# A two-headed SSM kernel on one core: inverse transform as 64 and 32 points, last stage on two groups at once, eight skips moved from TensorE to VectorE, and a new order of all work

## Chip, core and metric

The kernel runs on one core of one Trainium2 chip. The metric is the device time of one execution in microseconds (us). The engines are named as in the profile: PE (TensorE matmul; PEld its weight loads), DVE (VectorE), ACT (ScalarE), POOL (GpSimd) and SP (SyncE, which here only issues DMAs).

## What is computed

Two heads, whose outputs stand side by side. Head A is a diagonal complex recurrence over 2048 steps with 640 states; head B is a causal convolution over 2048 steps, done in the reference by FFT, of 640 channels, between two products.

```python
# A: x [1, 2048, 640]
Lam_bar = exp(dt * Lam);  B_bar = ((Lam_bar - 1) / Lam)[:, None] * Bmat
Bu = einsum("bld,pd->blp", x, B_bar)
h_t = Lam_bar * h_{t-1} + Bu_t                       # all t
a = 2 * einsum("blp,dp->bld", h, Cmat).real + x * Dskip
# B: q, k, v [1, 2048, 640]
kv = (sum of 4 shifted k * shift_k) * v
y = irfft(rfft(pad(kv, 4096)) * rfft(pad(ssm_k, 4096)))[:2048] + kv * ssm_D
b = q * y
out = concatenate([a, b], -1)                        # bfloat16
```

## The kernel before

**Head A.** Time is cut into 4 interleaved phases s (steps 4m + s), states into 5 blocks j of 128. `v{s}_{j}` (`pe_in`, L513) projects phase s of x, transposed as `xT{s}`, onto block j and adds the phase before it through diagonal matrices; `ve{s}_{j}` empties it from PSUM. Phase 0 then holds the input of a recurrence with a step of 4, which DVE does as a rotation (`rs`), a scan (`sc`) and a rotation back (`ra`, `rout`); `oa{s}_{j}` and `od{s}_{j}` carry its result to the other phases. `p{i}_{s}` (`pe_proj`, L571) is the output projection for rows i of phase s: two banks with 10 matmuls of 320 columns each, and then 3 small ones in each with a diagonal matrix of Dskip (`diagD`, L587), which add x * Dskip. `yo{i}_{s}` (L604) empties it on ACT, `yd{i}_{s}` (L607) stores it. C is brought in by two transposing DMAs (`CT0`, `CT1`) and scaled by `ca` (ACT) and `cs` (DVE).

**Head B.** Channels are cut into 5 groups G of 128. `kT`, `vT` are transposed loads; `tap` is the 4-step filter on PE, `kv` the product with v on DVE, `kvo` and `kvs` a trip to DRAM and back into another layout, `hs` the load of the filter's row (64 partitions at a time, pieces of 128 bytes). The transform runs in two stages: `s1h`/`s1k` (L662, 64 x 64 quarters of the array) and `s2h`/`s2k` (L675, two column halves), each emptied by `s1he`, `s1ke`, `s2he`, `s2ke`. `ya{G}_{half}` and `y{G}_{half}` (L687, L688, L693) are the product of the spectra on DVE. Then comes the way back. `inv{G}_{q}` (`pe_inv`, L695) takes 4 of 16 frequencies k1 with whole 128 x 128 matrices, four matmuls for each (real and imaginary part of in and out); `zs` empties 1024 columns into `Zs`; `zt{G}_{half}` (`turn_z`, L710) is a transposing DMA inside SBUF into `Zt`; `fin{G}_{half}` (`pe_fin`, L717) is the last stage, 16 matmuls with a moving matrix `Mq` of 64 columns; `ob{G}_{half}` (L725, DVE) multiplies by q, loaded by `qi{G}` (L715), and `od_{G}` (L730) stores the group.

**What sets the order.** `make_plan` gives each step its engine, its costs and what it needs; the costs steer nothing in the program that runs. `ORDER`, a list written out in full, is the sequence in which all steps are issued: each engine works through its own steps in this order and waits where a step's input is not there. `@n` names the PSUM bank pair, of which there are four, and a `!` puts a step on its other engine (an evacuation on DVE instead of ACT, a transposed copy on ACT, small parameters on POOL or SP).
SP's list is a queue too: a DMA whose input is late holds back all DMAs behind it.

Of the kernel before, what the change touches and what calls it, by code (L numbers as in the profile page):

```python
# [45 lines left out]
class Kernel:  # L46


    def __init__(self, ctx, tc, out, ins):
# [75 lines left out]
        t("qb", [128, 16, 128])  # L125
# [6 lines left out]
        self.Zt = self.zz[:, 4096:8192].rearrange("p (i b) -> p i b", i=32)  # L132
# [3 lines left out]
        self.tph = [flat(n).bitcast(i32).rearrange("p (q n) -> p q n", q=2) for n in (self.qb, self.kv_st)]  # L136
# [6 lines left out]
        self.diagG = self.H[:, 2].rearrange("p a b -> p (a b)")[:, 0:3 * n * 128].rearrange("p (s j d) -> p s j d", s=3, j=n)  # L143
# [46 lines left out]
    def pool_consts2(self):  # L190
# [3 lines left out]
        g.iota(self.c26[:], pattern=one, base=2 ** 26, channel_multiplier=0)  # L194
# [4 lines left out]
        g.iota(self.m_ph[:], pattern=[[1, 16]], base=0, channel_multiplier=0)  # L199

    def pool_consts3(self):
# [831 lines left out]
```

## Time and profile before

| What | Value |
|---|---|
| Median of 3 runs | 201.43 us (201.4 to 201.59) |
| The profiled execution | 201.36 us, its span 199.6 us |
| PE busy | 186.4 us (93%), weight loads 128.3 us |
| DVE busy | 164.9 us (83%) |
| ACT busy | 153.8 us (77%) |
| POOL busy | 24.8 us (12%) |
| DMA | 32.61 MB, mean 163 GB/s, 124908 packets, of them 120903 under 512 B |
| Longest waits | ACT for the projections (L604 on L587) 22.7 us in 10; DVE for the last stage (L725 on L720) 15.9 us in 2 |

The page calls an engine busy from the start of an instruction to its modelled end. Matmuls overlap in the pipeline: one of 128 columns reads as 219 ns, and the next begins 57 ns later. So the cost of a row of matmuls is read from the starts of what follows, not from the mean of one.

### The profile page before, as it was taken

What the parts mean: (1) busy time and instruction counts of PE and PEld (TensorE: products, weight loads), DVE (VectorE), ACT (ScalarE), POOL (GpSimd) and SP (SyncE); (2) the same over time, 40 slices, a digit from 0 to 9 for tenths busy, and PEclk for the clock granted to TensorE, in tenths of its full rate; (3) what the DMA queues carried; (4) which work ended last, traced back from release to release, by engine and by line L of the source; (5) the groups of instructions that cost most, each with busy time, mean ns of one, the idle gap of its engine ahead of it and who ended that gap; (6) DMA issues with size and microseconds to landing.
All of it is one profiled execution on the core that took longest, in us unless ns stands there. A gap on an engine that the chain in (4) does not pass through costs nothing. (4 is left out here: it accounts for less than half of the span.)

```text
span 199.6 us, 7503 instructions
## 1 busy us (share of the span) xinstructions
PE 186.4 (93%) x3328; PEld 128.3 (64%) x3340; DVE 164.9 (83%) x285; ACT 153.8 (77%) x189; POOL 24.8 (12%) x55
## 2 busy tenths in 40 slices
PE   7999999999989999999999998887999999999990
PEld 4444365544445456567777887677778887977770
DVE  5899877999999999999999999999999898420040
ACT  2499999988958998899998899799898983501321
POOL 8899561000000000000000000000000000000000
PEclk9999999999999999999999999999999999999998
DMA  4999999993586831985999786997995796597635
GB/s 112 209 221 217 207 266 214 210 192 85 90 174 163 164 50 27 240 163 86 236 188 194 121 167 126 157 254 140 194 155 150 158 164 153 126 175 176 143 130 138
DMA packets 124908, 32.61 MB, mean 163 GB/s; under 512 B 120903, under 2 KB 124236, under 8 KB 124876
## 3 DMA queue, kind: packets, MB, share of 16 engines
q1 hardware_dynamic: 124856, 32.13, 81.0%
q8 instruction: 26, 0.43, 0.9%
q14 instruction: 6, 0.05, 0.1%
q10 hardware_dynamic: 20, 0.01, 0.0%
HBM read 9.51 MB, written 7.86 MB: 87 GB/s over the span
## 5 line engine op out<-in xcount | busy, mean ns | idle before, releaser
L520 PE MATMUL ps<-xT,BT 128*128 128x512 bf16 x188 | 47.8, 381 | 0.9 <-DMA xT<-in_A_x_dram 0.3
L582 PE MATMUL ps<-Cs,hs 128*128 128x320 bf16 x240 | 36.3, 299 | 0.3 <-ACT Xs L467 0.3
L520 PEld LDWEIGHTS <-BT 128*128 128x128 bf16 x200 | 18.7, 98 | 22.6 <-issue 1.3
L604 ACT CAST BT<-ps 128x640 bf16<-128x640 f32 x16 | 10.9, 695 | 25.7 <-PE ps L587 22.7
L582 PEld LDWEIGHTS <-hs 128*128 128x128 bf16 x240 | 21.9, 98 | 7.9 <-issue 0.2
L725 DVE TENSOR_TENSOR qb<-ps,qb 128x1024 bf16<-128x1024 f32 x10 | 11.9, 1216 | 15.9 <-PE ps L720 15.9
L675 PEld LDWEIGHTS <-G 128*64 128x64 bf16 x640 | 19.1, 110 | 5.5 <-issue 4.1
L467 ACT CAST As_kv<-ps 128x1024 bf16<-128x1024 f32 x20 | 20.0, 1041 | 0.3 <-PE ps L662 0.3
L467 ACT CAST As_h<-ps 128x1024 bf16<-128x1024 f32 x20 | 19.8, 1040 | 0.0
L467 ACT CAST Hf<-ps 128x1024 bf16<-128x1024 f32 x19 | 19.3, 1042 | 0.0
L467 ACT CAST Xs<-ps 128x1024 bf16<-128x1024 f32 x19 | 18.8, 1031 | 0.0
L467 ACT CAST zz<-ps 128x1024 bf16<-128x1024 f32 x17 | 17.2, 1034 | 2.1 <-PE ps L704 2.1
L701 PE MATMUL ps<-Xs,H 128*128 128x128 bf16 x80 | 17.5, 219 | 0.9 <-ACT As_h L467 0.5
L703 PE MATMUL ps<-Xs,H 128*128 128x128 bf16 x80 | 17.5, 219 | 0.8 <-issue 0.8
L702 PE MATMUL ps<-Xs,H 128*128 128x128 bf16 x80 | 17.5, 219 | 0.4 <-DVE Xs L693 0.4
L704 PE MATMUL ps<-Xs,H 128*128 128x128 bf16 x80 | 17.5, 219 | 0.0
L693 DVE TENSOR_TENSOR Xs<-Xs,rot 128x1024 bf16<-128x1024 bf16 x20 | 12.9, 686 | 0.2
L687 DVE TENSOR_TENSOR rot<-Xs,Hf 128x2048 bf16<-128x2048 bf16 x10 | 12.2, 1220 | 0.8 <-ACT BT L604 0.5
L675 PE MATMUL ps<-As_kv,G 128*64 128x128 bf16 x320 | 11.7, 221 | 1.0 <-DVE vT L651 0.5
L688 DVE TENSOR_TENSOR Xs<-Xs,Hf 128x2048 bf16<-128x2048 bf16 x10 | 12.2, 1225 | 0.5
L675 PE MATMUL ps<-As_h,G 128*64 128x128 bf16 x320 | 11.7, 221 | 0.7 <-ACT Xs L467 0.7
L651 DVE TENSOR_TENSOR vT<-ps,vT 128x1024 bf16<-128x1024 f32 x10 | 11.9, 1213 | 0.4 <-PE ps L646 0.4
(204 smaller groups left out, 396.5 us busy)
## 6 DMA issues: line engine op xcount, KB each, us to landing
h_st<-in_B_ssm_k_dram SPq DMA_DIRECT2D x10, 256.0 KB, 4.2
kv_rows<-vT SPq DMA_DIRECT2D x5, 512.0 KB
kv_st<-kv_rows SPq DMA_DIRECT2D x10, 256.0 KB, 3.7
qb<-in_B_q_dram SPq DMA_DIRECT2D x5, 512.0 KB, 4.0
out_dram<-BT SPq DMA_DIRECT2D x16, 160.0 KB, 2.6
out_dram<-qb SPq DMA_DIRECT2D x5, 512.0 KB, 5.2
As_kv<-in_A_B_re_dram SPq DMA_DIRECT2D x3, 160.0 KB, 2.4
As_kv<-in_A_B_im_dram SPq DMA_DIRECT2D x3, 160.0 KB, 2.5
```

The source lines that it names most:

```text
L467: self.nc.scalar.copy(out=out, in_=in_)
L520: mm(o, lhsT=self.BT[:, r, k, j * 128:(j + 1) * 128], rhs=xT[:, k, :], start=(k == 0), stop=(s == 1 and k == NT - 1))
L582: mm(o[:, 0:320], lhsT=h[:, r, ts], rhs=self.Cs[:, r, j, c0:c0 + 320], start=(j == 0 and r == 0), stop=(not on_pe and j == NT - 1 and r == 1))
L651: self.nc.vector.tensor_tensor(out=self.vT[:, ts], in0=ps[:].rearrange("p a n -> p (a n)"), in1=self.vT[:, ts], op=ALU.mult)
L675: self.nc.tensor.matmul(o[64 * e:64 * e + 64, c:c + 128], lhsT=self.G[:, r, k, :], rhs=As[:, k, :], start=True, stop=True)
L687: tt(out=self.cross(), in0=X[:, ::-1, :], in1=self.Hf[:, 1:2, hs].to_broadcast([128, 2, 1024]), op=ALU.mult)
L688: tt(out=X, in0=X, in1=self.Hf[:, 0:1, hs].to_broadcast([128, 2, 1024]), op=ALU.mult)
L693: self.nc.vector.tensor_tensor(out=X[:, r, :], in0=X[:, r, :], in1=cr[:, r, :], op=ALU.add if r else ALU.subtract)
L701: mm(o_re, lhsT=self.H[:, 0, k1, :], rhs=yre, start=True, stop=False)
L702: mm(o_re, lhsT=self.H[:, 2, k1, :], rhs=yim, start=False, stop=True)
L703: mm(o_im, lhsT=self.H[:, 1, k1, :], rhs=yre, start=True, stop=False)
L704: mm(o_im, lhsT=self.H[:, 0, k1, :], rhs=yim, start=False, stop=True)
```

## The change

**The inverse** (`pe_inv`). The matrix `H` gets the layout [16 frequencies, 3, 64]: minus sine, cosine, sine of 64 points. Two neighbours of the three, 128 columns, are the weights of one matmul, which takes 64 rows of the spectrum (the even or the odd half e of the frequencies) and gives real and imaginary part for 64 points at once. Four matmuls for each k1 stay, each on half the rows; half e goes into its own PSUM bank. `zs` is now two copies of 512 columns. Half as many table entries are made (`H0`, `H1` in place of four), and the negated part is half as large. `diagG` gets a tile of its own instead of a part of `H`.

**The last stage** (`pe_fin`). `Mq` now has 2 x 32 x 4 entries, a real and an imaginary part with 32 points each. One piece takes 8 of the 32 blocks of `Zt` of two groups at once: the even group on column half 0 of the array, the odd one on column half 1, for each block and group two accumulating matmuls with 128 moving columns. Groups 0 and 1, and 2 and 3, go in four pieces together (`fin0_*`, `fin1_*`); group 4 goes alone in two (`fin2_*`), its channels split between the halves. For this `Zt` exists twice, the second time on top of `tabs`, whose last reader is `ra4`. `qb` holds two groups, 64 partitions each; loads and stores of q are 64 x 32 x 128 elements for a group, and for group 4 two DMAs of 64 x 32 x 64.

**The skips.** Eight projections, `SKV`, leave out the diagonal matmuls. For these x is loaded again, untransposed (`xs`, 160 KB each, three buffers), DVE multiplies it by Dskip (`xd`, bf16 in SBUF) and adds it when it empties PSUM (`yo` on DVE). The methods for this were there before and unused. The projections go in the order `PORD`; projection (1, 1) is done, emptied and stored by halves.

**The order.** `ORDER` is another list throughout. `lv3`, `lv1` and `lv4` (rows of parameters) go first on SP; `lam` and `gam` go to POOL.

```diff
+SKV = [(0, 1), (2, 3), (2, 0), (2, 1), (3, 3), (3, 2), (3, 1), (1, 3)]
+LAST = (1, 1)
-        t("H", [128, 3, 16, 128])
+        t("H", [128, 16, 3, 64])
-        t("qb", [128, 16, 128])
+        t("qb", [128, 32, 128])
-        self.Zt = self.zz[:, 4096:8192].rearrange("p (i b) -> p i b", i=32)
+        self.Zt = [f.rearrange("p (i b) -> p i b", i=32) for f in (self.zz[:, 4096:8192], tf[:, 0:4096])]
...
-        self.nc.vector.tensor_scalar_mul(out=self.H[:, 2], in0=self.H[:, 1], scalar1=-1.0)
+        self.nc.vector.tensor_scalar_mul(out=self.H[:, :, 0], in0=self.H[:, :, 2], scalar1=-1.0)
...
     def pe_inv(self, ks, ps):
-        mm = self.nc.tensor.matmul
+        for i, k1 in enumerate(ks):
+            for r in range(2):
+                for e in range(2):
+                    rows = slice(64 * e, 64 * e + 64)
+                    y = self.Xs[rows, k1 // 8, r, 128 * (k1 % 8):128 * (k1 % 8) + 128]
+                    self.nc.tensor.matmul(ps[:, e, 128 * i:128 * i + 128], lhsT=self.H[rows, k1, 1 - r:3 - r, :].rearrange("p o n -> p (o n)"),
+                                          rhs=y, start=(r == 0), stop=(r == 1))
+
+    def act_zs(self, ks, ps):
+        for e in range(2):
+            k = 16 * e + ks[0]
+            self.copy(self.Zs[:, :, k:k + 4].rearrange("p i k c -> p k i c"), ps[:, e].rearrange("p (k i c) -> p k i c", k=4, c=4))
...
+    def qo(self, eng, G, load):
+        for x in (range(2) if G == NG - 1 else (None,)):
+            g, c0, n = (G % 2, 128 * G, 128) if x is None else (x, 128 * G + 64 * x, 64)
+            b = self.qb[64 * g:64 * g + 64, :, 0:n]
+            d = (self.q2[:, c0:c0 + n] if load else self.o2[:, D + c0:D + c0 + n]).rearrange("(a b) c -> b a c", b=64)
+            if load:
+                eng.dma_start(out=b, in_=d)
+            else:
+                eng.dma_start(out=d, in_=b)
+
+    def pe_fin(self, G, q, ps):
         psf = ps[:].rearrange("p a n -> p (a n)")
...
-        for i in range(16):
-            self.nc.tensor.matmul(psf[:, 64 * i:64 * i + 64], lhsT=self.Zt[:, 16 * hf + i, :],
-                                  rhs=self.Mq[:].rearrange("p a c -> p (a c)"), start=True, stop=True)
+        for i in range(8):
+            for r in range(2):
+                for h in range(2):
+                    g, j = (0, 16 * h + 8 * q + i) if G == NG - 1 else (h, 8 * q + i)
+                    self.nc.tensor.matmul(psf[64 * h:64 * h + 64, 128 * i:128 * i + 128], lhsT=self.Zt[g][:, j, 64 * r:64 * r + 64],
+                                          rhs=self.Mq[:, r].rearrange("p a c -> p (a c)"), start=(r == 0), stop=(r == 1))
...
 ORDER = """
-lv1! pc lsk lv0! lv4 B0 pc2 dc dc3 wm0@0 lv2! zer lv3! pc3 dc2 wm1@2 B1 gp1 dsel x1 tsk@4 gp0 bt0@6 tske@4 dS0 tv@0 wm2@2 pp
+lv3! pc lsk lv1! lv0 lv4! lv2 pc2 dc B1 dc3 wm0@0 zer pc3 B0 dc2 wm1@2 pk x1 dsel tsk@4 gp1 tv@6 tske@4 tve@6 bt1@0 gp0 kT0 den
...
```

Three places in the order carry the prediction. The first is SP's queue near its beginning, from the first transposed load of x on (x1, then x2, x3 and last x0). Before, where x0 and the loads of C come later still:

```order
L182 DMA_TRANSPOSE xT_136<-in_A_x_dram 128x5x512
L182 DMA_TRANSPOSE xT_137<-in_A_x_dram 128x5x512
L182 DMA_TRANSPOSE xT_138<-in_A_x_dram 128x5x512
L613 DMA_TRANSPOSE vT<-in_B_v_dram 128x2048
L176 DMA Xs<-in_A_B_re_dram 128x640
L176 DMA Xs<-in_A_B_im_dram 128x640
L613 DMA_TRANSPOSE kT<-in_B_k_dram 128x2048
```

and now:

```order
L184 DMA_TRANSPOSE xT_134<-in_A_x_dram 128x5x512
L617 DMA_TRANSPOSE kT<-in_B_k_dram 128x2048
L184 DMA_TRANSPOSE xT_135<-in_A_x_dram 128x5x512
L846 DMA_TRANSPOSE Cs<-in_A_C_re_dram 128x5x640
L184 DMA_TRANSPOSE xT_136<-in_A_x_dram 128x5x512
L846 DMA_TRANSPOSE Cs<-in_A_C_im_dram 128x5x640
L184 DMA_TRANSPOSE xT_133<-in_A_x_dram 128x5x512
L617 DMA_TRANSPOSE vT<-in_B_v_dram 128x2048
L178 DMA As_kv<-in_A_B_re_dram 128x640
```

Both loads of C and the load of k have moved ahead of x0 and of v; the loads of B for blocks 2 to 4, of which two stood among them, all follow behind v.

The second place is the end of DVE's queue, from the second product of group 4's spectra (`ya4_0`, `y4_0`). Before:

```order
L687 TENSOR_TENSOR rot<-Xs,Hf 128x2048
L688 TENSOR_TENSOR Xs<-Xs,Hf 128x2048
L693 TENSOR_TENSOR Xs<-Xs,rot 128x1024 x2
L465 CAST zz<-ps_64 128x8x32x4
L725 TENSOR_TENSOR qb<-ps_65,qb 128x16x64
```

and now:

```order
L692 TENSOR_TENSOR Xs<-Xs,Hf 128x2048
L697 TENSOR_TENSOR Xs<-Xs,rot 128x1024 x2
L603 TENSOR_TENSOR BT<-ps_67,BT 128x640
L738 TENSOR_TENSOR qb<-ps_65,qb 128x32x32
L738 TENSOR_TENSOR qb<-ps_67,qb 128x32x32
L738 TENSOR_TENSOR qb<-ps_66,qb 128x32x32
L738 TENSOR_TENSOR qb<-ps_65,qb 128x32x32
L599 TENSOR_TENSOR BT<-BT 128x640
L603 TENSOR_TENSOR BT<-ps_67,BT 128x640
L603 TENSOR_TENSOR BT<-ps_64,BT 128x640
L603 TENSOR_TENSOR BT<-ps_66,BT 128x640
```

Where one evacuation of the inverse and four products with q stood behind the last product of spectra, there are now four products for groups 2 and 3, and the sums of five projections (L603) with the products they need (L599); two products for group 4 follow. On PE, behind the same point, stand two pieces of the inverse, three of the last stage (groups 2 and 3), p2_1, p3_3, p3_2, p3_1, the two halves of p1_1, two pieces of the last stage (group 4) and p1_3; before, three pieces of the inverse, three of the last stage and seven projections.

The third place is the end of SP's queue, from the last transposes inside SBUF. Before:

```order
L712 DMA_TRANSPOSE zz<-zz 128x16x128 x2
L730 DMA out_dram<-qb 128x16x128
L607 DMA out_dram<-BT 128x640
L715 DMA qb<-in_B_q_dram 128x16x128
L607 DMA out_dram<-BT 128x640 x5
L730 DMA out_dram<-qb 128x16x128
L607 DMA out_dram<-BT 128x640
```

and now:

```order
L725 DMA out_dram<-qb 64x32x128 x2
L715 DMA_TRANSPOSE zz<-zz 128x16x128
L593 DMA BT<-in_A_x_dram 128x640
L723 DMA qb<-in_B_q_dram 64x32x64 x2
L611 DMA out_dram<-BT 128x640
L593 DMA BT<-in_A_x_dram 128x640
L611 DMA out_dram<-BT 128x640
L611 DMA out_dram<-BT 128x320
L611 DMA out_dram<-BT 128x640
L611 DMA out_dram<-BT 128x320
L611 DMA out_dram<-BT 128x640
L725 DMA out_dram<-qb 64x32x64 x2
```

The load of q for group 4 (L723) now stands behind two stores of whole groups, one transpose and one load of x, and the last group's store is two DMAs in place of one; a store of a projection is still the last.

More of the change, by code (lines that the diff above doesn't have):

```diff
@@ L920, in make_plan @@
+            A(f"zs{G}_{q}", "ACT", 0.98, [f"inv{G}_{q}"] + ([f"zt{G - 1}_0", f"zt{G - 1}_1"] if pre else xts_all),
+              lambda ps, q=q: K.act_zs(range(4 * q, 4 * q + 4), ps), give=f"inv{G}_{q}", alt=("DVE", 1.17))
+        last, P = G == NG - 1, G // 2
         for hf in range(2):
-            turn(f"zt{G}_{hf}", 2.9, [f"zs{G}_{q}" for q in range(4)] + ([f"fin{G - 1}_{hf}"] if pre else xts_all + cs_all),
-                 lambda hf=hf: K.turn_z(hf))
-        dma(f"qi{G}", "SP", 0.42, 2.9, [f"od_{G - 1}"] if pre else Hs + [f"tab{j}" for j in J], lambda e, G=G: K.load_q(e, G))
@@ L924, in make_plan @@
[L924 to L927 removed]
+            old = [f"fin{P - 1}_{q}" for q in (2 * hf, 2 * hf + 1)] if P > 0 else xts_all + cs_all + [f"ra{j}" for j in J] * G
```

209 lines of the change are left out of this document (104 added, 105 removed).

## The prediction

> **What bounds the kernel now.** I read the page's head first, then busy time by stretches of 20 us, then the timeline of VectorE (DVE), then TensorE (PE) from 150 us on, and last the chain that ended last.
>
> ```profile
> span 199.6 us, 7503 instructions
> 40.00:60.00 20.00, 19.30 (x354) 9.65 (x355) 19.62 (x36) 15.89 (x18) 0.00 (x0) 1.00 0.71 135
> 100.00:120.00 20.00, 19.87 (x473) 16.17 (x472) 19.62 (x34) 18.00 (x22) 0.00 (x0) 1.00 0.94 165
> 120.00:140.00 20.00, 16.86 (x532) 14.30 (x526) 19.65 (x30) 18.59 (x21) 0.00 (x0) 1.00 0.91 171
> 160.00:180.00 20.00, 19.63 (x268) 15.97 (x265) 12.10 (x12) 8.10 (x10) 0.00 (x0) 1.00 0.83 156
> 180.00:199.60 19.60, 14.84 (x154) 11.20 (x152) 2.35 (x2) 4.65 (x7) 0.00 (x0) 0.96 0.56 144
> ```
>
> Columns after the length: PE, PE's weight loads, DVE, ACT, POOL, granted clock, DMA share, GB/s. The mean over the page says "PE"; the stretches say something else. From 40 to 140 us DVE is busy 19.6 of every 20 us, as full as PE or fuller. Only after 160 does DVE empty out and PE work alone. So there are two regimes: up to the last product of group 4 (y4_0) DVE decides, behind it PE.
>
> ```profile
> 29.86 2.36 DVE L651 TENSOR_TENSOR vT<-ps,vT 128x1024 bf16<-128x1024 f32 x2 [0.44 <-PE ps L646]
> 33.84 1.22 DVE L465 CAST z<-ps 128x1024 bf16<-128x1024 f32 x1 [1.03 <-PE ps L523]
> 157.63 1.22 DVE L465 CAST Hf<-ps 128x1024 bf16<-128x1024 f32 x1 [0.84 <-PE ps L675]
> 168.31 1.29 DVE L693 TENSOR_TENSOR Xs<-Xs,rot 128x1024 bf16<-128x1024 bf16 x2
> 169.66 0.22 PE L702 MATMUL ps<-Xs,H 128*128 128x128 bf16 x1 [0.37 <-DVE Xs L693]
> 194.87 0.69 ACT BT L604
> 193.84 0.38 SPq L730 DMA_DIRECT2D out_dram<-qb  x1
> SPq L1028 <- DMA out_dram<-qb: 1.8, 1, 1.8
> ```
>
> DVE runs from kv0 at 29.86 to the end of y4_0 at 168.31 + 1.29 = 169.60 with hardly a wait; PE is stopped for that product (the 0.37), then needs 194.87 - 169.60 = 25.27 us for what is queued behind it. The last store of group 4 (od_4) goes out at 193.84, and the queue's end waits 1.8 for it: the span closes 5.76 us after that issue.
>
> **The change part by part: PE.** Prices from PE's own rows, as starts of consecutive groups:
>
> ```profile
> 150.61 0.71 PE L662 MATMUL ps<-R,kv_st 64*64 64x64 bf16 x64
> 151.25 0.64 PE L675 MATMUL ps<-As_h,G 128*64 128x128 bf16 x16
> 152.37 0.22 PE L701 MATMUL ps<-Xs,H 128*128 128x128 bf16 x1
> 156.01 0.63 PE L720 MATMUL ps<-Mq,zz 128*128 128x64 bf16 x16
> 156.57 0.45 PE L662 MATMUL ps<-R,kv_st 64*64 64x64 bf16 x32
> 160.22 1.08 PE L675 MATMUL ps<-As_kv,G 128*64 128x128 bf16 x32
> 161.68 1.53 PE L582 MATMUL ps<-Cs,h 128*128 128x320 bf16 x10
> 167.69 0.63 PE L720 MATMUL ps<-Mq,zz 128*128 128x64 bf16 x16
> 168.16 0.22 PE L701 MATMUL ps<-Xs,H 128*128 128x128 bf16 x1
> 174.27 0.14 PE ps L587 x3
> 174.41 1.36 PE ps L582 x10
> ```
>
> Inverse, before: 64 matmuls from 152.37 to 156.01, 0.057 each, 16 in 0.91. Final stage, before: 16 in 168.16 - 167.69 = 0.47. From it to a stage of another shape (156.57 - 156.01 = 0.56) costs 0.09 more; I use 0.1 per change of shape. By the order, PE changes shape 70 times in both kernels (row halves, column halves, quarters, whole array counted as four kinds), so that is a wash. Two column halves side by side: the 32 matmuls of the row at 160.22 and the 16 behind them (48 in all) end at 161.68, less one change 1.36, 0.028 each. Four quarters: 64 in 0.64.
>
> The new inverse is 16 matmuls on row halves (64 rows, 128 columns, 128 moving). No row shows this shape. Bounds: 0.91 if the halves do not overlap, 0.45 if they overlap like the column halves. The quarters' row shows row halves overlapping too, so I take 0.46: 20 x -0.45 = -9.0 us. The new final stage is ten pieces of 32 matmuls in the very form of the row at 160.22 (128*64, 128 moving): 0.91 each, 9.1 in place of 4.7, +4.4. Eight projections lose their diagonal matmuls, 2 x 0.14 each: -2.2. PE in sum: -6.8 us.
>
> [...]
>
> **DVE.** Only what stands between kv0 and y4_0 moves y4_0.
>
> ```profile
> L725 DVE TENSOR_TENSOR qb<-ps,qb 128x1024 bf16<-128x1024 f32 x10 | 11.9, 1216 | 15.9 <-PE ps L720 15.9
> L539 DVE TENSOR_TENSOR rot<-rot 128x512 bf16<-128x512 bf16 x10 | 3.8, 422 | 0.2
> L568 DVE TENSOR_TENSOR rot<-rot,hs 128x1024 bf16<-128x1024 bf16 x10 | 6.8, 684 | 0.0
> L451 DVE SCALAR_TENSOR_TENSOR Cs<-Cs,gam,zz 128x640 bf16<-128x640 bf16 x2 | 1.8, 885 | 0.1
> L634 DVE TENSOR_TENSOR diagS<-id,sk_b 128x512 bf16<-128x512 bf16 x5 | 3.4, 686 | 0.0
> ```
>
> Out of that stretch go cs0 and cs1 (four instructions like the L451 row: -3.54), one dS (-0.69), half of the negated table (about -0.34) and two of the six products with q that stood there (-2.44). They are paid ahead of kv0, where DVE loses lam, gam and three evacuations. In come one evacuation more (seven for six, +1.22), five skips x*D (640 wide, between 422 and 684: 0.49 each, +2.45) and two sums out of PSUM (640 of the 1024 of L725, 0.76 by width, 0.80 with a fixed part: +1.60). Sum: -1.74. PE's freed 6.8 us hardly count here; what frees y4_0 is 1.7 us of DVE.
>
> [...]
>
> ACT is not the bound: it loses eight evacuations and two quarters of table, and pays two halves for each zs, a fraction of a us each.
>
> **The start.** These rows carry it:
>
> ```profile
> 3.94 9.07 SPq L182 DMA_TRANSPOSE xT<-in_A_x_dram  x3
> 13.06 2.56 SPq L613 DMA_TRANSPOSE vT<-in_B_v_dram  x1
> 25.47 3.03 SPq L836 DMA_TRANSPOSE Cs<-in_A_C_re_dram  x1
> 35.38 4.08 SPq L836 DMA_TRANSPOSE Cs<-in_A_C_im_dram  x1
> 9.65 4.71 PE L520 MATMUL ps<-xT,BT 128*128 128x512 bf16 x19 [0.28 <-DMA xT<-in_A_x_dram]
> vT<-in_B_v_dram SPq DMA_TRANSPOSE x5, 4.4
> ```
>
> SP issues its transposes back to back, 3.0 each for x. Now one small load fewer stands ahead of x1 (0.3 earlier), but kT0 and both C transposes (7.1 us) come ahead of x0, vT0 and three pairs of B. Adding the durations, vT0 is issued at about 26.1 and lands at 30.5, 0.6 later than kv0 began; B2 lands near 32, just as PE comes to bg0. Against this, the wait of 1.03 after kv0 goes (v0_1 is evacuated early). I book the start at 0, bounds -0.4 and +1.5. So y4_0 ends at 169.60 - 1.74 = 167.9.
>
> **The end.** Behind y4_0 PE now has two inverse pieces (0.92), five final pieces (4.55), five projections without diagonal (13.6), one with (3.0) and six changes of shape (0.6): 22.7 instead of 25.3. PE ends at 190.6, its last final piece 2.8 earlier, 187.8. That piece follows another by 0.9 and each has its product on DVE: 186.9 + 0.2 + 2 x 1.22 = 189.5 is when od_4 is issued (193.84 before). It is cut in two DMAs of 64 x 32 x 64 elements, 256 KB each, the form of h_st's load:
>
> ```profile
> h_st<-in_B_ssm_k_dram SPq DMA_DIRECT2D x10, 256.0 KB, 4.2
> 28.54 2.01 SPq L627 DMA_DIRECT2D h_st<-in_B_ssm_k_dram  x2
> out_dram<-qb SPq DMA_DIRECT2D x5, 512.0 KB, 5.2
> ```
>
> The second starts 1.0 after the first and lands 4.2 (like h_st) to 5.2 (like a whole store) later; 5.2 is nearer, as it is a store, but both ends of 10.4 (two whole stores in turn) stay in the range. 189.5 + 1.0 + 5.2 = 195.7. Before, landing by that row was 193.84 + 5.2 = 199.04 and the span ended 0.56 later: 196.3 now. The profiled execution took 201.36, 1.76 more than its span; the median of three is 201.43. Forecast: 196.3 + 1.76 = **198.0 us**, 1.7% less.
>
> **The rivals.**
>
> 1. PE's whole saving arrives (DVE's waits shrink, PE sets the pace): 201.36 - 6.8 = 194.6. For it: PE idles most in 120 to 140 (16.86 busy). Against: DVE is at 19.65 there.
> 2. The row halves do not overlap, or their weight loads hold them at the old pace. Up to y4_0 PE's idle time hides most of it; behind it two pieces cost 0.9 more, and one group's four in front of y4_0 up to 1.8: 198.9 to 200.7, say 199.5. Against it stands the quarters' row.
> 3. DVE's strict queue gets new waits for PE: the products ob0_2 and ob0_3, the sum yo2_0 and the skips now stand among the kv and y steps of groups 2 and 3, and PE itself waits at p3_0 for rout4, which comes late on DVE. Everything behind a waiting evacuation is late, and DVE has nothing to give. Each us goes to the end one for one; from 3.4 us on the kernel is slower. The worst wait of that kind was this one:
>
> ```profile
> 172.53 1.22 DVE L465 CAST zz<-ps 128x1024 bf16<-128x1024 f32 x1 [2.93 <-ACT zz L467]
> ```
>
>    Two such, 5.9 us: 203.9. Against: the old order had 3 us of such waits in 140.
> 4. The new order gives back what the counts free, through the later vT0 and B2 and the last q load, which waits on SP behind two stores: 201.4.
>
> **How the numbers follow.** Forecast 0.55, rival 1 0.12, rival 2 0.08, rival 3 0.20, rival 4 0.05. The forecast's own range is 196.5 (od_4 like h_st, start at its good end) to 200.5 (start late, od_4 as two stores for half of it). For 8 in 10 it goes down to 195.0, which leaves out most of rival 1, and up to 202.5, into rival 3. A difference under 0.2% is no change here. Faster 0.75 (forecast, rivals 1 and 2), same 0.05, slower 0.20.
>
> **What would show it.** In the changed profile: inverse groups 0.46 apart per 16 and final ones 0.91 per 32; y4_0's end near 168 and kv0 near 30; PE behind it 22.7 us without a stop; od_4 issued near 189.5. Wrong would be: y4_0 before 165 (PE had been the bound), inverse at 0.9, DVE waits over 5 us between kv0 and y4_0, or od_4 landing 8 us or more after issue.

## The result, and the profile after

The changed kernel takes 208.53 us in the median of four runs (208.02 to 208.87), the kernel before 201.42 beside it: a ratio of 1.035 (95% interval 1.033 to 1.038), so slower by 7.1 us where 3.4 us of gain were forecast. The profiled execution took 208.58 us with a span of 206.7; the forecast's span was 196.3, so 10.4 us are to be explained. Ratios here and below leave disturbed runs out, medians keep them.

The head of the page after (columns as before):

```profile
span 206.7 us, 7773 instructions
PE 182.6 (88%) x3452; PEld 121.4 (59%) x3452; DVE 172.0 (83%) x285; ACT 149.4 (72%) x197; POOL 26.7 (13%) x66
PEclk9999999999999999999999999999979999999996
q1 hardware_dynamic: 130414, 33.60, 94.7%
q8 instruction: 27, 0.44, 0.9%
```

PE did become cheaper in busy time (186.4 before), ACT too (153.8 before); DVE has 7.1 us more by what it took over, and POOL 1.9. Two rows are new. The time of the data queue q1's packets adds up to 94.7% of the time of the 16 DMA engines (81.0% before) for 4.6% more bytes. This share is no fill level: in the stretches below it reaches 1.50 at 118 GB/s, so it counts packets that overlap or wait. And the clock falls once in mid-span, at slice 30 of 40.

The stretches of 20 us show where (columns: PE, weight loads, DVE, ACT, POOL, clock, DMA share, GB/s):

```profile
120.00:140.00 20.00, 19.07 (x579) 15.35 (x577) 19.58 (x28) 18.56 (x25) 0.00 (x0) 1.00 1.06 193
140.00:160.00 20.00, 13.69 (x425) 10.48 (x427) 14.85 (x21) 13.57 (x18) 0.00 (x0) 0.91 1.09 167
160.00:180.00 20.00, 18.00 (x469) 14.98 (x458) 17.18 (x19) 12.90 (x19) 0.00 (x0) 1.00 0.88 147
```

From 140 to 160 us PE, DVE and ACT are all idle, each for 5 to 6.4 us: none of the three is the bound there. DVE's timeline, from kv0 to the end of y4_0, tells what it waited for; these are its only waits over 0.3 us in those 144 us:

```profile
30.60 2.35 DVE L655 TENSOR_TENSOR vT<-ps,vT 128x1024 bf16<-128x1024 f32 x2
...
140.75 0.31 DVE L634 TENSOR_TENSOR h_st<-h_st,dcol_b 128x32 bf16<-128x32 bf16 x1 [0.51 <-DMA h_st<-in_B_ssm_k_dram]
151.03 1.23 DVE L691 TENSOR_TENSOR rot<-Xs,Hf 128x2048 bf16<-128x2048 bf16 x1 [1.17 <-ACT Xs L469]
156.38 0.82 DVE L603 TENSOR_TENSOR BT<-ps,BT 128x640 bf16<-128x640 f32 x1 [1.53 <-PE ps L584]
159.93 1.29 DVE L467 CAST zz<-ps 128x512 bf16<-128x512 f32 x2 [1.59 <-PE ps L705]
164.25 1.23 DVE L467 CAST Hf<-ps 128x1024 bf16<-128x1024 f32 x1 [1.91 <-PE ps L679]
173.35 1.29 DVE L697 TENSOR_TENSOR Xs<-Xs,rot 128x1024 bf16<-128x1024 bf16 x2
```

They sum to 6.7 us (2.7 before, in four), and y4_0 ends at 173.35 + 1.29 = 174.64. That this is 6.7 later than forecast as well is chance. DVE's busy time over the whole stretch from kv0 to the end of y4_0, before and now, gives the account (length of the stretch, DVE's busy time and count, clock, DMA share, GB/s):

```profile
29.86:169.60 139.74, 134.34 (x201) 1.00 0.82 158
30.60:174.65 144.05, 134.04 (x205) 0.99 1.00 158
```

DVE's idle time, short gaps included, rose from 5.4 to 10.0 us, and its work fell by 0.3 us where 1.74 were forecast. So the 6.7 us are 0.7 of a later start, 4.6 of idle time and 1.4 of work that did not go away.

Of the five waits all but 0.51 is for PE, or for ACT, which had waited for PE. And PE, in its own timeline, waited longest for nothing that the profile names:

```profile
136.50 1.01 PE L705 MATMUL ps<-Xs,H 64*128 64x128 bf16 x30 [0.65 <-issue]
140.77 0.44 PE L666 MATMUL ps<-R,kv_st 64*64 64x64 bf16 x30 [0.43 <-issue]
146.69 0.98 PE L666 MATMUL ps<-R,h_st 64*64 64x64 bf16 x94 [2.24 <-issue]
152.07 4.27 PE L584 MATMUL ps<-Cs,hs 128*128 128x320 bf16 x18 [2.42 <-issue]
163.51 1.14 PE L679 MATMUL ps<-As_h,G 128*64 128x128 bf16 x34 [1.24 <-issue]
```

Together 7.0 us of "issue" (0.8 before). The stalls end in the middle of a step, on whatever matmul comes next. What they have in common is seen by counting instructions between their ends: matmuls first (busy time, count, clock, DMA share, GB/s).

```profile
136.49:140.76 4.27, 3.63 (x128) 1.00 0.82 200
140.76:146.68 5.92, 3.58 (x128) 1.00 1.11 173
146.68:152.06 5.38, 2.62 (x128) 1.00 1.50 118
152.06:159.10 7.04, 6.37 (x125) 0.76 0.84 178
```

And the weight loads in the first three of these stretches:

```profile
136.49:140.76 4.27, 3.23 (x128) 1.00 0.82 200
140.76:146.68 5.92, 3.32 (x128) 1.00 1.11 173
146.68:152.06 5.38, 2.07 (x128) 1.00 1.50 118
```

128 matmuls and 128 loads from one stall to the next: 256 instructions, as many as one packet of q8, the instruction queue, holds (0.44 MB in 27 packets are 16 KB each, and 27 x 256 = 6912 for PE's 6904). PE had run out of instructions and waited for the next block. The same count holds beyond this kernel: in the 15 profiles of this study PE has 42 issue stalls over 0.35 us, and counted in PE's records, the ends within one kernel all lie multiples of 256 apart, give or take two. In the three stretches above, a block's packet starts 1.9 to 3.0 us after PE has begun the block ahead of it, takes 0.9 to 1.6 us, and PE goes on 1.3 to 1.8 us later: 4.3 to 5.9 us a block, while PE works off 128 short pairs in 3.6. Why a packet here starts only when PE has begun the block ahead, the runs do not show. The forecast did not weigh how fast the blocks come.

The second part of the miss stands behind y4_0: 32.1 us to the end of the span, 28.4 forecast, 30.0 before.

```profile
191.68 2.19 SPq L723 DMA_DIRECT2D qb<-in_B_q_dram  x2
193.58 0.49 DVE L599 TENSOR_TENSOR BT<-BT 128x640 bf16<-128x640 bf16 x1 [5.31 <-DMA BT<-in_A_x_dram]
198.24 2.35 DVE L738 TENSOR_TENSOR qb<-ps,qb 128x1024 bf16<-128x1024 f32 x2 [3.25 <-DMA qb<-in_B_q_dram]
200.62 1.69 SPq L725 DMA_DIRECT2D out_dram<-qb  x2
```

od_4 goes out at 200.62 in place of 189.5: 6.7 us because y4_0 is late, 3.25 because its product waits for the last load of q, and 1.1 in smaller pieces. The list of DMAs, now:

```profile
qb<-in_B_q_dram SPq DMA_DIRECT2D x4, 512.0 KB, 8.6
out_dram<-qb SPq DMA_DIRECT2D x4, 512.0 KB, 8.2
```

Before, these rows had 4.0 and 5.2. They are no averages of all transfers: the profile tells the landing of few. The 8.6 is one load, the first of two issued together at 44.21; the 4.0 is one load near the end, at 183.62.

### The profile page after: what moved, and what is told of

The parts are those of the page before. It is cut to its first block, busy times and chain, and to the rows that moved or that the text cites. A ratio compares the mean times of both kernels' runs of the same rounds, so it can differ in the third digit from the quotient of the medians.

```text
span 206.7 us, 7773 instructions
## 1 busy us (share of the span) xinstructions
PE 182.6 (88%) x3452; PEld 121.4 (59%) x3452; DVE 172.0 (83%) x285; ACT 149.4 (72%) x197; POOL 26.7 (13%) x66
## 3 DMA queue, kind: packets, MB, share of 16 engines
q1 hardware_dynamic: 130414, 33.60, 94.7%
## 4 chain that ended last, share of the span: by engine, by line
PE 42%; ACT 17%; DMA 12%; SPq 10%; DVE 9%; issue 7%; DVEq 0%; ACTq 0%
PE ps L522 12%; PE ps L584 12%; SPq L184 5%; PE ps L679 4%; DMA kT<-in_B_k_dram 3%; PE ps L705 3%; DMA Cs<-in_A_C_im_dram 3%; DMA kv_st<-kv_rows 3%; DMA qb<-in_B_q_dram 3%; ACT zz L469 3%; PE ps L666 3%; ACT kS L625 2%; ACT Hf L469 2%; PE ps L525 2%; PE ps L524 2%
## 5 line engine op out<-in xcount | busy, mean ns | idle before, releaser
L522 PE MATMUL ps<-xT,BT 128*128 128x512 bf16 x200 | 48.7, 379 | 1.7 <-DVE hs L467 0.9
L584 PEld LDWEIGHTS <-hs 128*128 128x128 bf16 x240 | 23.0, 100 | 12.5 <-issue 3.0
L469 ACT CAST BT<-ps 128x640 bf16<-128x640 f32 (+3 forms) x13 | 9.4, 735 | 20.5 <-PE ps L589 20.5
L469 ACT CAST zz<-ps 128x512 bf16<-128x512 f32 x38 | 19.6, 614 | 0.9 <-PE ps L705 0.9
L469 ACT CAST Hf<-ps 128x1024 bf16<-128x1024 f32 x18 | 18.2, 1045 | 1.2 <-PE ps L679 1.2
L469 ACT CAST As_kv<-ps 128x1024 bf16<-128x1024 f32 x18 | 17.9, 1046 | 0.6 <-PE ps L666 0.6
L705 PE MATMUL ps<-Xs,H 64*128 64x128 bf16 x320 | 11.4, 217 | 1.3 <-issue 0.7
L603 DVE TENSOR_TENSOR BT<-ps,BT 128x640 bf16<-128x640 f32 x8 | 6.6, 823 | 6.5 <-PE ps L584 6.2
L551 DVE TENSOR_TENSOR_SCAN z<-rr,rot 128x512 bf16<-128x512 f32 x10 | 11.7, 1207 | 0.0
L584 PE MATMUL ps<-Cs,h 128*128 128x320 bf16 x80 | 11.5, 300 | 0.0
```

What stands on the lines that cost most here:

```text
L469: self.nc.scalar.copy(out=out, in_=in_)
L522: mm(o, lhsT=self.BT[:, r, k, j * 128:(j + 1) * 128], rhs=xT[:, k, :], start=(k == 0), stop=(s == 1 and k == NT - 1))
L551: self.nc.vector.tensor_tensor_scan(out=self.zt(j)[:, r, :], data0=rb, data1=self.rot_p[:, r, :], initial=0.0, op0=ALU.mult, op1=ALU.add)
L584: mm(o[:, 0:320], lhsT=h[:, r, ts], rhs=self.Cs[:, r, j, c0:c0 + 320], start=(j == 0 and r == 0), stop=(not on_pe and j == NT - 1 and r == 1))
L705: self.nc.tensor.matmul(ps[:, e, 128 * i:128 * i + 128], lhsT=self.H[rows, k1, 1 - r:3 - r, :].rearrange("p o n -> p (o n)"), rhs=y, start ...
```

## The experiments

The table has for each kernel the median of its runs, and from its profile the stretch from kv0 to the end of y4_0, the stretch from there to the end of the span, and the sum of PE's issue stalls over 0.35 us behind 100 us. Medians of the kernel before in these runs were 201.5 to 201.8. Executions of one kernel in the new order scatter by 0.9 to 5.3 us, those of before by 0.6 to 2.1. The last three columns come from one execution each, and it is not always near the median: time_halves was profiled at 209.5, q_over_128_q4_early at 207.4, q4_early at 208.0. So differences of 1 us between two profiles are weak evidence.

| Kernel | Time, us | Ratio to before (95%) | kv0 to y4_0 | y4_0 to end | PE stalls |
|---|---|---|---|---|---|
| before | 201.4 | | 139.7 | 30.0 | 0.8 |
| forecast | 198.0 | | 138.0 | 28.4 | |
| changed | 208.5 | 1.035 (1.033 to 1.038) | 144.0 | 32.1 | 7.0 |
| q_over_128 | 205.1 | 1.011 (1.007 to 1.015) | 144.2 | 28.0 | 5.5 |
| q4_early | 209.8 | 1.039 (1.034 to 1.044) | 142.2 | 32.8 | 4.8 |
| q_over_128_q4_early | 205.1 | 1.015 (1.011 to 1.019) | 143.9 | 29.5 | 2.7 |
| time_halves | 206.3 | 1.021 (1.017 to 1.025) | 146.4 | 28.1 | 7.7 |
| before_split | 205.1 | 1.017 (1.013 to 1.021) | 143.6 | 30.1 | 2.9 |
| after_merged | 208.6 | 1.034 (1.030 to 1.038) | 144.1 | 32.1 | 4.6 |
| q_over_128_merged | 202.6 | 1.000 (0.997 to 1.004) | 141.9 | 28.1 | 1.7 |
| no_skip_loads | 206.2 | 1.022 (1.019 to 1.025) | 143.3 | 29.8 | 4.3 |
| all_three | 199.7 | 0.989 (0.985 to 0.993) | 138.8 | 27.6 | 1.7 |
| before_half_inverse | 202.4 | 1.004 (1.001 to 1.007) | 140.7 | 29.5 | 1.4 |
| before_skips | 201.8 | 1.001 (0.999 to 1.003) | 140.1 | 29.3 | 0 |
| skips_back | 208.3 | 1.033 (1.027 to 1.038) | 143.2 | 33.1 | 4.9 |
| before_q64 | 202.7 | 1.006 (1.004 to 1.008) | 140.1 | 30.7 | 0.6 |

My first theory was the transfers of q alone. Four runs went out on it.

**q_over_128.**

```diff
-            b = self.qb[64 * g:64 * g + 64, :, 0:n]
+            b = self.qb[:, 16 * g:16 * g + 16, 0:n]
-            d = (self.q2[:, c0:c0 + n] if load else self.o2[:, D + c0:D + c0 + n]).rearrange("(a b) c -> b a c", b=64)
+            d = (self.q2[:, c0:c0 + n] if load else self.o2[:, D + c0:D + c0 + n]).rearrange("(a b) c -> b a c", b=128)
```

> Of the changed kernel only the shape of the q transfers is altered: each load and store of q lies over 128 partitions with 16 rows, as before the change, in place of 64 partitions with 32 rows; bytes, packets, order and arithmetic instructions stay (the products pair with q of other times, so the outputs of head B are not the reference's). Theory T (the 64-partition q transfers are the cause: they take about twice the ring time, so other loads and the instruction fetch come late): q load lands in 4 to 5 us (8.6 in the changed kernel), q1 share 84 to 88% (94.7), PE's issue stalls of 2.2 to 2.4 us gone, y4_0 ends at 167 to 170 (174.6), time 199 to 203. Rival R1 (the new order of SP's queue and the skip loads crowd the rings, the shape does not matter): y4_0 still ends after 173, time 206.5 to 209. Rival R2 (what is lost is the last q load's place alone): y4_0 unchanged, tail 1 to 2 us shorter, time 206 to 207.5.

Measured: 205.1. From its list of queues and DMAs:

```profile
q1 hardware_dynamic: 130414, 33.60, 90.1%
qb<-in_B_q_dram SPq DMA_DIRECT2D x4, 512.0 KB, 7.3
out_dram<-qb SPq DMA_DIRECT2D x4, 512.0 KB, 6.3
```

In the profile the whole gain lies behind y4_0: 28.0 us, near the 28.4 forecast. In front of it the stretch is as long as in the changed kernel, and 5.5 us of stalls stayed. So the shape bears on the second part of the miss and not on the first, and the theory fell as the only cause. The q load of 7.3 is again the first of two that this order issues at once, right behind kvs1.

**q4_early**, and both together.

```diff
-            b = self.qb[64 * g:64 * g + 64, :, 0:n]
+            b = (self.h_st if G == NG - 1 else self.qb)[64 * g:64 * g + 64, :, 0:n]
...
 ORDER = """
-fin1_2@2 ob1_0@4 zt4_0 p2_1@6 ob1_2@2 xd3_3 od_2 p3_3@0 yo2_1@6 od_3 p3_2@4 yo3_3@0 zt4_1 p3_1@2 yo3_2@4 xs3_1 qi4 p1_1a@6 yd2_1
+fin1_2@2 ob1_0@4 qi4 zt4_0 p2_1@6 ob1_2@2 xd3_3 od_2 p3_3@0 yo2_1@6 od_3 p3_2@4 yo3_3@0 zt4_1 p3_1@2 yo3_2@4 xs3_1 p1_1a@6 yd2_1
```

> Of the changed kernel only group 4's q is altered: it has a buffer of its own (h_st, which is dead by then) and its two loads are issued ahead of zt4_0 instead of behind od_2, od_3, zt4_1 and xs3_1. Theory T: the tail behind y4_0 was 32.1 us, 3.7 more than forecast, because ob2 waited 3.25 us for this load; y4_0 stays at 174 to 175, ob2 no longer waits for qb, time 204 to 206. Rival R2 (the last q load is all that was lost): the same size here, 204 to 206, but then nothing is left for the shape. Rival R3 (PE and the stores set the tail anyway, 18.4 us without a stop): time 207.5 to 209.

> Both edits of the two runs ahead together (outputs of head B again not the reference's). Theory T: the two losses (6.7 us ahead of y4_0, 3.7 behind it) go both, time 196 to 200, near the forecast of 198.0. R1: 204 to 206. R2: as q4_early, 204 to 206.

Measured: 209.8 and 205.1; q4_early gains nothing, by itself or on top of q_over_128. In DVE's timeline of q4_early the wait has only changed its name:

```profile
195.54 0.49 DVE L599 TENSOR_TENSOR BT<-BT 128x640 bf16<-128x640 bf16 x1 [8.55 <-DMA BT<-in_A_x_dram]
196.12 0.82 DVE L603 TENSOR_TENSOR BT<-ps,BT 128x640 bf16<-128x640 f32 x1
196.87 2.35 DVE L738 TENSOR_TENSOR h_st<-ps,h_st 128x1024 bf16<-128x1024 f32 x2
```

The load of q is there, but the product stands in DVE's queue behind a skip, which waits 8.55 us for its load of x, issued behind the transpose zt4_1. Moving this one load ahead only makes room for the next late one.

**time_halves**, a whole kernel with q over 128 partitions (each load and store of q one DMA, as before the change).

```diff
-        for i in range(8):
+        g, hf = (0, q) if G == NG - 1 else (q % 2, q // 2)
+        for i in range(16):
...
-                    self.nc.tensor.matmul(psf[64 * h:64 * h + 64, 128 * i:128 * i + 128], lhsT=self.Zt[g][:, j, 64 * r:64 * r + 64],
-                                          rhs=self.Mq[:, r].rearrange("p a c -> p (a c)"), start=(r == 0), stop=(r == 1))
+                    self.nc.tensor.matmul(psf[64 * h:64 * h + 64, 64 * i:64 * i + 64], lhsT=self.Zt[g][:, 16 * hf + i, 64 * r:64 * r + 64],
+                                          rhs=self.Mq[:, r].rearrange("p (a h) c -> p h a c", h=2)[:, h], start=(r == 0), stop=(r == 1))
```

> A whole kernel: q over 128 partitions again, each q piece of the final stage handles one group's half with its 64-row column halves taking alternate blocks of 64 times, so 64 products of 64 columns in place of 32 of 128. Theory T: the transfers as in q_over_128; the 64 products cost 0.91 us a piece if two column halves overlap at 14 ns each, 1.8 us if each takes the 28 ns of a 64-column load; with 10 pieces that is 0 to +9 us of PE, so 199 to 206. R1: 206.5 or more.

Measured: 206.3. A piece costs 1.0 to 1.2 us of PE (0.9 to 1.0 in the changed kernel), but the kernel has 640 PE instructions more, and the stalls grew to 7.7 us. The tail is 28.1 again, the stretch ahead of y4_0 the longest of all. That turned me to theory F, the supply of instructions; the next runs change the number of PE instructions and leave PE's time alone.

**before_split.**

```diff
-            mm(o_re, lhsT=self.H[:, 0, k1, :], rhs=yre, start=True, stop=False)
-            mm(o_re, lhsT=self.H[:, 2, k1, :], rhs=yim, start=False, stop=True)
...
+            for o, hs in enumerate(((0, 2), (1, 0))):
+                for r in range(2):
+                    for c in range(2):
+                        self.nc.tensor.matmul(psf[64 * c:64 * c + 64, 256 * i + 128 * o:256 * i + 128 * o + 128],
+                                              lhsT=self.H[:, hs[r], k1, 64 * c:64 * c + 64], rhs=y[r], start=(r == 0), stop=(r == 1))
```

> Of the kernel before only the products of the inverse are altered: each of 128 columns becomes two of 64 columns (the result is the same), so a piece has 32 products and 32 weight loads in place of 16 and 16, at the 28 ns that 64-column products take in place of 57: the same 0.91 us of PE, but 640 PE instructions more, about 2.5 blocks of 16 KB on the instruction queue. Theory F (PE is held up by the supply of its instructions: in the changed kernel the stalls named issue end at every 256th PE instruction, 4.3 to 5.9 us after the one before, in the stretch where short products follow one another): PE gets issue stalls of 1 to 3 us in the stretch from 125 to 165 us, and the time is 203 to 208. Rival R1 (the order of the changed kernel and its transfers are the cause, the number of instructions is not): 201 to 202, no issue stall over 1 us.

Measured: 205.1. The old order, the old transfers, the same work on the same time of PE, and yet 3.4 us slower. Its PE timeline:

```profile
135.65 0.22 PE L662 MATMUL ps<-R,h_st 64*64 64x64 bf16 x2 [1.85 <-issue]
151.08 0.29 PE L662 MATMUL ps<-R,h_st 64*64 64x64 bf16 x12 [1.01 <-issue]
```

Here are the stalls of the changed kernel, in a kernel that has nothing of it but denser instructions. kv0 to y4_0 grew by 3.9 us, the tail not at all. F holds: the supply of instructions alone can cost this much.

**after_merged** and **q_over_128_merged**, the second with the edit of q_over_128 as well.

```diff
-                for e in range(2):
-                    rows = slice(64 * e, 64 * e + 64)
-                    y = self.Xs[rows, k1 // 8, r, 128 * (k1 % 8):128 * (k1 % 8) + 128]
-                    self.nc.tensor.matmul(ps[:, e, 128 * i:128 * i + 128], lhsT=self.H[rows, k1, 1 - r:3 - r, :].rearrange("p o n -> p (o n)"),
-                                          rhs=y, start=(r == 0), stop=(r == 1))
+                y = self.Xs[:, k1 // 8, r, 128 * (k1 % 8):128 * (k1 % 8) + 128]
+                self.nc.tensor.matmul(ps[:, r, 128 * i:128 * i + 128], lhsT=self.H[:, k1, 1 - r:3 - r, :].rearrange("p o n -> p (o n)"),
+                                      rhs=y, start=True, stop=True)
...
-                for h in range(2):
-                    g, j = (0, 16 * h + 8 * q + i) if G == NG - 1 else (h, 8 * q + i)
-                    self.nc.tensor.matmul(psf[64 * h:64 * h + 64, 128 * i:128 * i + 128], lhsT=self.Zt[g][:, j, 64 * r:64 * r + 64],
-                                          rhs=self.Mq[:, r].rearrange("p a c -> p (a c)"), start=(r == 0), stop=(r == 1))
+                g, j = (0, 16 * r + 8 * q + i) if G == NG - 1 else (r, 8 * q + i)
+                self.nc.tensor.matmul(psf[:, 128 * i:128 * i + 128], lhsT=self.Zt[g][:, j, :],
+                                      rhs=self.Mq[:, r].rearrange("p a c -> p (a c)"), start=(r == 0), stop=(r == 1))
```

> Of the changed kernel only the products of the inverse and of the final stage are altered: two of half the rows or half the columns become one of 128 by 128, so 8 and 16 products a piece in place of 16 and 32, at 57 ns in place of 28: the same 0.46 and 0.91 us of PE, 640 PE instructions fewer (the sums mix halves, so the outputs of head B are not the reference's). Theory F: the issue stalls of 2.24, 2.42 and 1.24 us fall below 1 us each, y4_0 ends at 168 to 170.5 (174.6), time 202 to 205. R1: 207.5 to 209, y4_0 after 173.

> The run ahead with q over 128 partitions as well. Theory F with the transfers' share: q_over_128 gained 3.4 us, mostly behind y4_0; here 198.5 to 201.5. R1: as q_over_128, 204.5 to 206.

Measured: 208.6 and 202.6. By itself the edit gave nothing, against F. The timeline of after_merged shows why, in one row of PE and one of DVE:

```profile
165.92 0.88 PE L679 MATMUL ps<-As_kv,G 128*64 128x128 bf16 x18 [3.29 <-issue]
166.24 0.49 DVE L599 TENSOR_TENSOR BT<-BT 128x640 bf16<-128x640 bf16 x1 [2.54 <-DMA BT<-in_A_x_dram]
```

The stalls at 147 and 152 had fallen below 1 us and y4_0's chain led the changed kernel by 2.9 us at 162. Then both a block of instructions and a load of x came late at the same moment, behind the stores od_0 and od_1: this block's packet started 4.6 us after the block ahead of it had begun. With q over 128 partitions the same block costs 1.04:

```profile
164.30 0.69 PE L679 MATMUL ps<-As_kv,G 128*64 128x128 bf16 x18 [1.04 <-issue]
```

So the two causes are not separate terms. How dense the instructions are says how soon a block is needed; the data transfers around it say how late it comes, as far as one block in two profiles can show. With both eased the kernel is level with before, above the 198.5 to 201.5 expected. Its longest wait left on DVE (2.25 us at 159.12) goes back not to a block but to a transpose inside SBUF, for which ACT had waited 2.83.

**no_skip_loads** and **all_three** (the edits of q_over_128_merged and this one).

```diff
     def load_xs(self, eng, i, s, n):
+        return
```

> The changed kernel without the eight loads of x for the skips (what lies in the buffers is multiplied instead, so eight blocks of head A are not the reference's); 1.3 MB less, all else the same. Theory F: the fetches start a little sooner, the stalls shrink by some tenths each, the tail gains as xs3_1 and xs1_3 are not waited for: 205 to 207.5. R1 (these loads crowd out the others): 201 to 204.

> The changed kernel with q over 128 partitions, 640 PE instructions fewer at the same PE time, and without the eight loads of x (outputs of head B and eight blocks of head A not the reference's). Theory S (the miss is the ring: q's shape, the added loads, and PE's instruction blocks that wait behind both; the forecast's PE and DVE terms hold): kv0 to the end of y4_0 138 to 140.5 (141.9 in q_over_128_merged, 144.0 in the changed kernel, 137.6 forecast), time 198 to 200.5. Rival R1 (the order itself leaves DVE waits behind, whatever the ring does): y4_0 141.5 or more behind kv0, time 201.5 to 203.

Measured: 206.2 and 199.7. With the transfers and the instructions eased on all three sides, the stretches of the forecast come back:

```profile
31.26 2.35 DVE L656 TENSOR_TENSOR vT<-ps,vT 128x1024 bf16<-128x1024 f32 x2
...
160.93 0.69 PE L680 MATMUL ps<-As_kv,G 128*64 128x128 bf16 x18 [1.73 <-issue]
162.30 1.23 DVE L692 TENSOR_TENSOR rot<-Xs,Hf 128x2048 bf16<-128x2048 bf16 x1 [1.59 <-ACT Xs L469]
168.74 1.29 DVE L698 TENSOR_TENSOR Xs<-Xs,rot 128x1024 bf16<-128x1024 bf16 x2
```

kv0 to y4_0 is 138.8 us (138.0 forecast) and the tail 27.6 (28.4 forecast); the one wait over 0.3 us left on DVE is again a block of instructions. Over this stretch, DVE's busy time is:

```profile
31.26:170.03 138.77, 133.77 (x205) 1.00 0.93 158
```

So DVE is idle for 5.0 us of it, as little as before, and the order as such leaves nothing behind: R1 falls. From 208.5 the steps are 3.4 (q's shape), 2.5 (640 instructions), 2.9 (1.3 MB of x); taken alone, in the same sequence, 3.4, 0 and 2.3.

**before_half_inverse**: what is PE time in the inverse worth in the old order?

```diff
-            mm(o_re, lhsT=self.H[:, 0, k1, :], rhs=yre, start=True, stop=False)
-            mm(o_re, lhsT=self.H[:, 2, k1, :], rhs=yim, start=False, stop=True)
-            mm(o_im, lhsT=self.H[:, 1, k1, :], rhs=yre, start=True, stop=False)
-            mm(o_im, lhsT=self.H[:, 0, k1, :], rhs=yim, start=False, stop=True)
+            for o in range(2):
+                y = self.Xs[:, k1 // 8, o, 128 * (k1 % 8):128 * (k1 % 8) + 128]
+                self.nc.tensor.matmul(psf[:, 256 * i + 128 * o:256 * i + 128 * o + 128], lhsT=self.H[:, o, k1, :], rhs=y,
+                                      start=True, stop=True)
```

> The kernel before with half of the products of the inverse left out (one of two sums for each part, so head B is not the reference's): 0.46 us a piece in place of 0.91 and 320 PE instructions fewer, in the order of before. The forecast's two regimes: nothing ahead of y4_0 (its end stays at 169 to 170, since DVE decides there), 4 pieces behind it give 1.8 us: 199.2 to 200.2. Rival (PE decides all along, 20 pieces count): 193 to 197.

Measured: 202.4, outside the 199.2 to 200.2 expected: some 9 us of PE less (20 x 0.45) give no gain. Ahead of y4_0 that was forecast. Behind it 0.5 us arrived and not 1.8, since PE then waits between its inverse pieces for y and for the evacuations (1.1 us in four waits), and ahead of y4_0 1.0 us was lost, where PE has this stall:

```profile
134.37 0.69 PE L717 MATMUL ps<-Mq,zz 128*128 128x64 bf16 x10 [1.38 <-issue]
```

The rival in which PE decides all along is out by 5 us.

**before_skips** and **skips_back** take the skips alone, on either side.

```diff
-SKV = []
+SKV = [(1, 3), (1, 1), (2, 1), (2, 3), (3, 1)]
...
-p1_1@6 yo1_3@2 yd1_3 p2_1@2 yo1_1@6 qi4 yd1_1 p3_1@6 yo2_1@2 yd2_1 yo2_3@0 yd2_3 fin4_1@2 yo3_1@6 fin4_0@0 ob4_1@2 yd3_1 p3_2@6
+p1_1@6 yo1_3@2 yd1_3 xs2_3 p2_1@2 yo1_1@6 qi4 yd1_1 xs3_1 xd2_3 p3_1@6 yo2_1@2 yd2_1 yo2_3@0 yd2_3 fin4_1@2 xd3_1 yo3_1@6 fin4_0@0 ob4_1@2 yd3_1 p3_2@6
```

(`Db` goes behind kvo4, `xs1_3`, `xs1_1` and `xs2_1` behind qi2, their products behind ob3_0.) And of the changed kernel, where every `Db`, `xs` and `xd` leaves the list:

```diff
-SKV = [(0, 1), (2, 3), (2, 0), (2, 1), (3, 3), (3, 2), (3, 1), (1, 3)]
+SKV = []
...
-oa2_2 s2h1_3@0 Db ve0_4@4 od2_2 inv0_0@2 xs0_1 xs2_3 s2he1_3@0 tap2_0@6 xs2_0 rs4 zs0_0@2 s1k1_1@4 tap2_1@0 s1ke1_1@4 zt0_0
+oa2_2 s2h1_3@0 ve0_4@4 od2_2 inv0_0@2 s2he1_3@0 tap2_0@6 rs4 zs0_0@2 s1k1_1@4 tap2_1@0 s1ke1_1@4 zt0_0
...
```

> A whole kernel: the kernel before, its order and arithmetic kept, but the skips of five projections behind y4_0 (p1_3, p1_1, p2_1, p2_3, p3_1) go to DVE, which idles 15 us there, with five loads of x and one of D. PE loses 5 times 0.27 = 1.35 us behind y4_0 and 60 instructions; if the loads land in time and the ring is not in the way: 199.8 to 200.6. If od_4 and the last stores wait for the loads as in the changed kernel: 201.5 to 204.

> A whole kernel: the changed kernel with its eight skips back on PE (48 products, 96 PE instructions more), without the eight loads of x and the one of D. If the loads cost what no_skip_loads gave (2.3 us) and PE pays 0.27 us a skip, of which five lie behind y4_0 (1.35 us): 207 to 208.5, so the skips by DVE are worth nothing in this kernel. Rival (the skips by DVE gain what the forecast took for them, 2.2 us of PE): 209.5 to 211. If the ring counts for more than PE: 205.5 to 207.

Measured: 201.8 (before beside it 201.7) and 208.3. In before_skips PE's last matmul came 24.4 us behind y4_0 in place of 25.2, but y4_0 itself was 0.4 later and the end did not move. In the changed kernel undoing the skips changes nothing either, although DVE then has 2.9 us less to do between kv0 and y4_0 (131.1): it is idle for 2.1 us more. Both ways round the move is worth nothing. That the loads take back what PE is spared fits no_skip_loads (2.3 us) but is not shown by itself.

**before_q64**: q's shape alone, in the old order (two small tables move into `zz` to make room).

```diff
-        eng.dma_start(out=self.qb[:], in_=self.q2[:, 128 * G:128 * G + 128].rearrange("(a b) c -> b a c", b=128))
+        if G == 0:
+            self.nc.gpsimd.memset(self.qb[:], 0.0)
+        eng.dma_start(out=self.qb[64 * (G % 2):64 * (G % 2) + 64], in_=self.q2[:, 128 * G:128 * G + 128].rearrange("(a b) c -> b a c", b=64))
...
-        eng.dma_start(out=self.o2[:, D + 128 * G:D + 128 * G + 128].rearrange("(a b) c -> b a c", b=128), in_=self.qb[:])
+        eng.dma_start(out=self.o2[:, D + 128 * G:D + 128 * G + 128].rearrange("(a b) c -> b a c", b=64), in_=self.qb[64 * (G % 2):64 * (G % 2) + 64])
```

> The kernel before with only the shape of q's transfers altered, to 64 partitions with 32 rows, one group in the upper and the next in the lower half, as in the changed kernel (one group at a time, as before; rows of the other half are not multiplied, so head B is not the reference's). If the shape itself costs ring time: a q load lands in 6 to 8 us (4.0 before), q1 share 88 to 93% (81.0), and PE gets issue stalls over 1 us: 202.5 to 205. If the shape costs only in the changed kernel, where two such loads run at once behind kvs1's: a q load in 4 to 5 us, share below 85%, 201 to 202.2.

Measured: 202.7, 0.6% slower (0.4 to 0.8%).

```profile
q1 hardware_dynamic: 124856, 32.13, 82.4%
qb<-in_B_q_dram SPq DMA_DIRECT2D x5, 512.0 KB, 5.3
out_dram<-qb SPq DMA_DIRECT2D x5, 512.0 KB, 6.0
```

Between the two expectations: the shape by itself costs 1.3 us a load (the same one, near the end) and 0.8 a store. At the place of the changed kernel's load, the first of two behind other transfers, q_over_128 has 7.3 with the old shape and the changed kernel 8.6: 3.3 for the place and again 1.3 for the shape. The runs do not say why half the partitions take longer for the same packets.

No whole kernel of this study beats the one before; all_three does by 1.1%, and leaves work out.

## Why the prediction was wrong, step by step

- **The prices of the matmuls were right.** In the changed kernel 32 matmuls of the inverse (L705) begin at 173.05 and the last stage (L733) follows at 174.05: 0.45 for 16 after 0.1 for the change of shape; 0.46 was taken, and rival 2 is out. PE's busy time fell by 3.8 us in place of 6.8; the lowered clock alone gave back 1.9 of it at 152.07 (see the end).
- **The two regimes were right, and rival 1 falls**: before_half_inverse shows PE's time ahead of y4_0 to be worth nothing in the old order.
- **"PE's freed 6.8 us hardly count here; what frees y4_0 is 1.7 us of DVE" is the step that failed.** It took for granted that PE would keep up, since it had time to spare, and priced PE in microseconds of matmul only. PE had a second resource, its instructions, of which the change asks more (6904 in place of some 6,680) in less time. What showed in its place: 7.0 us of issue stalls on PE, DVE idle for 10.0 us in place of 5.4, y4_0 at 174.64 in place of 167.9. The 1.7 us of DVE were wrong as well: its work fell by 0.3 (0.6 in all_three). 0.8 of the difference is one rotation, L541 at 35.4, which took 1.22 us in place of 0.42; why, and where the rest went, stays open. In 14 of the 15 profiles DVE's work in this stretch is 133.8 to 134.5 us, so its idle time sets the length. Rival 3 had the form of it, new waits for PE in DVE's strict queue (3.4 us as the point from which it decides, 5.9 as its price), but blamed the sequence of steps; in all_three the same sequence waits 1.6 us, in one wait.
- **The start** was booked at 0, with bounds of -0.4 and +1.5: kv0 came 0.7 late, and 0.7 to 3.4 late over the kernels in the new order.
- **Behind y4_0, PE's 22.7 us held** (23.2 measured, 22.5 in all_three). **"186.9 + 0.2 + 2 x 1.22 = 189.5 is when od_4 is issued" failed**: it had PE's last piece as the last input of ob2, and took a landing time from each row of before without asking what else the DMA engines were to carry at that time. The load of q was the last input, by 3.25 us. Rival 4 named it, "the last q load, which waits on SP behind two stores", and had it too cheap.
- By part: 0.7 us from the start, 6.0 from kv0 to y4_0 (4.6 idle, 1.4 of DVE's work), 3.7 behind it. Undoing q's shape takes back all of the 3.7, leaving out the loads of x 2.3, so these two overlap. Of the 6.0, q_over_128_merged takes back 2.2 and all_three 5.3.
- **The range** does not quite follow from its own terms: 198.0 - 1.0 - 0.4 is 196.6, and 198.0 + 1.5 + 2.1 is 201.6, where 196.5 and 200.5 stand. Nothing hangs on it; the measured time lies beyond either.

## What to carry to other kernels

Replacing long matmuls by short ones can save PE time while it keeps or raises the number of instructions (here 3.8 us less of busy time, and 6904 instructions in place of some 6,680). Divide a stretch's matmuls and weight loads by 256 and ask whether a block can come that often (here one took 4.3 to 5.9 us in the crowded stretch), before any of the saved time is booked. A wait named "issue" in the middle of a step, with 256 instructions between one and the next, was that limit here. Work moved from an engine to a load was not free here: in both orders the skips gained nothing (201.8 us with them against 201.7 in the old one, 208.5 against 208.3 in the new). So add up the transfers of the whole stretch and do not rely on the landing time of one row.

## What the hardware showed that was not expected

- PE's instructions come during the run, in packets of 16 KB on a DMA queue (q8), beside the data's. A block took 4.3 to 5.9 us from the start of the one ahead to PE's next matmul in the crowded stretch, and once, in after_merged, its packet started only after 4.6 us.
- A stall cost more than itself here: after those at 146.69 and 152.07 the granted clock was 0.76 on the mean from 152.06 to 159.10, and the 18 projection matmuls at 152.07 took 4.27 us in place of 18 x 0.136 = 2.4. The trace has the clock at half for 3.41 us, from the end of the second stall on. It fell after 2.24 and 2.42 us of idle time, with work in between; in skips_back, with six stalls of up to 1.69 us, it did not fall before the last matmuls were done (0.996 over the whole run). What makes it fall, the runs do not show.
- Kernels whose beginning is the same instruction for instruction began kv0 between 30.6 and 33.2 us in the new order; in the old order it was 29.86 to 29.93 in every profile. The runs do not say why.
